# Turning the output and a token-major copy with VectorE's 32 x 32 transpose and 128-byte DMA pieces, instead of TensorE, in a fused attention and token/channel mixing kernel

## The chip, the cores and the metric

One Trainium2 chip, one core of it. The metric is the device time of one execution in microseconds (us); lower is better. The engines are written as in the profile: PE is TensorE, DVE is VectorE, ACT is ScalarE, POOL is GpSimd and SP is SyncE, which here issues nearly all DMAs.

## The reference

Two parts, one behind the other. Each of B = 8 batches has 8 heads, 1152 positions and head width 64. Queries are averaged in pairs, so there are 576 pooled queries per head.

```python
q_pool = q.reshape(B, H, S // 2, 2, D).mean(axis=3)
scores = matmul(q_pool, k^T) / sqrt(D)
attn = softmax(scores)                       # sum + 1e-9
x = (attn @ v) as [B, 576, H * D = 512]

theta = x @ w_theta                          # [576, 512] per batch
zr, zi = x * cos(theta), x * sin(theta)
y = w_tok_r @ zr + w_tok_i @ zi              # mixes the 576 tokens
u = x + y
out = u + max(u @ w_ch, 0)                   # mixes the 512 channels
```

Everything is float32. The kernel splits operands into a rounded high part and a rest (`hi` and `lo`, `xh` and `xl`, two `wth`, two `wtk`, two `wch`, two `us`) and multiplies three combinations, to keep float32 accuracy with a rounded format.

## The kernel before

**Phase 1** runs 32 pairs i = (batch b, head pair hp), two heads at a time, some 25 us each, to about 835 us. For pair i PE computes the score maxima (`pm`, L537; DVE reduces each with L544), the scores (`pe`, L622; ACT takes the exponential, L625), the sums of the exponentials (POOL adds them up, L636; PE collapses them in `pn`, L685) and the product with v (`pa`, L657; ACT copies it to `xu`, L669). `xu` is channel-major: 128 channels of two heads on the partitions, 576 tokens along the row. SP stores it to a DRAM tensor `xd[b]` (`norm_store`, L751). The copy of the row sums `sm` (L695, L697) goes to DRAM too (`norm_spread`, `sd<-sm`, L707), is inverted there in small tiles, and comes back as `rd`.

The schedule is written out by hand: `at(position, priority, function)` makes a list of steps, 18 units per pair, which is sorted, and each engine runs its instructions in the order of the list. A pair begins with a burst (`u = 0`): `prep_all` makes the operands of pair i + 2 (ACT `hi`, DVE `lo`, L524), then PE runs the products with v of the pair's first half. On DVE a weight-preparation step (`ws` L789, `wf` L791) stands behind `lo` in 18 of the pairs, and then come the pair's max reduces (`mx<-pm`).

PSUM in phase 1 is one pool of four two-bank tiles with tag `e`, so each new tile waits for the reader of the tile four allocations before it.

**Phase 2** handles the 8 batches in sequence with a period of some 57 us, again in an order written out by hand (`at2`, 56 units per batch). Per batch: `xT` (x by channel) is loaded from `xd`, scaled by the reciprocal sums (`xscale`, L240, with `dn` loaded from `rd`) and split into `xh` and `xl`. For each of up to five blocks j of 128 tokens `theta` (L297) runs 12 matmuls, and `xturn` (L285) turns the block of `xT` to token-major with four PE transposes into another PSUM bank; `chain` copies that to `xn` on ACT (L331), forms sine and cosine on DVE and ACT (`r`, `ab`), multiplies them with `xn` on DVE (L343), and rounds the products into `Z` (ACT L368, POOL L374). `token_mix` (L1055) multiplies the token weights with Z. `uadd` (L1071) adds x on DVE, giving `uT`, channel-major; `uhi` and `ulo` (L1077, L1081) split it into the tiles `us`; `channel` (L1096) multiplies with `wch`, and `relu` (L1108) adds the positive part into `uT`.

The output is wanted token-major. `oturn` (L1119) turns `uT` with 20 PE transposes per batch (five token blocks, four channel blocks) into PSUM, `ocopy` (L1137, ACT) copies it to SBUF, and `ostore` (L1143) writes whole rows to the output. For batches 0 to 6 these steps stand between the matmuls of the next batch.

Of the kernel before, what the change touches and what calls it, by code (L numbers as in the profile page):

```python
# [62 lines left out]
PAIRS = {"e": 4}  # L63
# [35 lines left out]
OT_AT = (58.2, 58.21, 58.22, 69.55, 69.56)  # L99
OT_AT6 = (58.2, 58.21, 58.22, 65.0, 65.01)  # L100
OT_LAG = (1.0, 1.0, 4.3, 1.0, 1.0)
OT_BANK = "rrtrr"
OT_LAST = "htmmr"
CH_LAST = ("mr", "mr", "mm", "mh")
CH_BANK = "mrmr"
TINY = 2.0**-15
# [9 lines left out]
def pooled_attention_moe_kernel(  # L116
# [50 lines left out]
    xd = [dram.tile([DM, SQ], F32, name=f"xd{b}") for b in range(B)]  # L167
    sd = [dram.tile([2 * H, HALF], F32, name=f"sd{b}") for b in range(B)]
# [5 lines left out]
    def bank2(kind, name):  # L174
        return ps.tile([P, 2, 512], F32, tag=kind, name=name, bufs=PAIRS[kind])

# [46 lines left out]
    def dload(b, c):  # L223
        if b == 1:
            if c == 0:
                shape = [P, H // 2, SQ]
                bst[b]["dns"] = pools["up"].tile(shape, F32R, tag="us0", name="dn1", bufs=1)
            dn = bst[b]["dns"][:, c].bitcast(F32)
        else:
            dn = dnp.tile([P, 5 * P], F32, tag="dn", name=f"dn{b}_{c}", bufs=2)  # L230
# [19 lines left out]

    chains = itertools.count()

    def turned(b, j):
        turn = bst[b].setdefault("turn", {})
        if j not in turn:
            if b == 0 and j < AHEAD:
                both = bank2("e", f"pq{j}")
                turn[j] = both[:, 0], both[:, 1]
            else:
                n = TURN0.index(j) - AHEAD  # L260
                th = bank("mhr"[n] if b == 0 else "h", f"pth{b}_{j}")
                turn[j] = th, bank("mtr"[n] if b == 0 else "t", f"pxn{b}_{j}")
# [39 lines left out]
    def chain(b, j):  # L302
# [27 lines left out]
        xn = tmp("xn")  # L330
        nc.scalar.copy(xn, st["xn", j])  # L331
# [52 lines left out]
    with ExitStack() as p1:  # L384
# [24 lines left out]
        if WARM:  # L409
            warm = bank2("e", "pwarm")  # L410
            for n in range(WARM):
                nc.tensor.matmul(warm[:, n % 2, 0:P], ident, ident, start=True, stop=True)

        state = {}

# [60 lines left out]
        def prep_t(i, g):  # L476
            st = state[i]
            kn = st["kn"]
            pt = st["pt", g] = bank2("e", f"pt{g}_{i}")
# [48 lines left out]
        def maxpass(i):  # L528
# [4 lines left out]
            for j in range(4):  # L533
                for g in range(3):
                    pm = bank2("e", f"pm{i}_{j}{g}")
# [10 lines left out]
                    )  # L546
                    yield

        def max_tail(i, pt):
            st = state[i]  # L550
            hi, tl, mx = st["hi"], st["tail"], st["mx"]
            pm = bank2("e", f"px{i}")
# [5 lines left out]
            if pt is None:  # L558
                pt = bank2("e", f"py{i}")
# [5 lines left out]
        def max_tail_red(i):  # L565
# [3 lines left out]
            nc.vector.tensor_reduce(mx[:, 8, 2:3], st["pt8"][:, 0, 3 * P :], AX.X, ALU.max)  # L569

# [19 lines left out]
        def first_row(i):  # L590
            px = bank2("e", f"pmt{i}")
            max_row(i, px)
            max_copy(i, px)

# [10 lines left out]
        def escore(i, u, kt):  # L605
# [4 lines left out]
            pe = bank2("e", f"pe{i}_{u}{kt}")  # L610
# [14 lines left out]
            nc.scalar.activation(pcs[u, kt], pe[:, :, 0:HALF], AF.Exp, scale=SC)  # L625

# [23 lines left out]
        def av(i, u):  # L650
# [3 lines left out]
            pa = bank2("e", f"pa{i}_{u}")  # L654
# [15 lines left out]
            if more:  # L670
                max_copy(i + 1, pa)

        def norm_sum(i, px):
# [22 lines left out]
            else:  # L696
                nc.scalar.activation(sm, px[:, 1, 0:HALF], AF.Identity, bias=eps)  # L697

# [26 lines left out]
        def prep_all(i, g):  # L725
# [5 lines left out]
            if g == 1:  # L731
                prep_tail(i)

        def tail_prep(i):
# [10 lines left out]
            if more:  # L745
                prep_lo(i + 3, 0)

# [7 lines left out]
        def weights():  # L755
# [79 lines left out]
            def finish_token(raw, kb, jt):  # L835
# [4 lines left out]
                pw2 = bank2("e", "pwt")  # L840
# [16 lines left out]
                for dst, src in (  # L857
# [6 lines left out]
                    split(dst[0], dst[1], src, nc.scalar, nc.vector)  # L864

# [62 lines left out]
        def plan(i):  # L928
# [42 lines left out]
            for n, fn in (  # L971
# [3 lines left out]
                at(base + pl[n], 9, fn, i)  # L975

        for i in range(NPAIR):
            plan(i)
        at(NU * NPAIR + 2, 9, lambda: norm_sum(NPAIR - 1, bank2("e", "pend")))
# [32 lines left out]
    with ExitStack() as p2:  # L1012
        for n, kinds in enumerate(BANKS2):
            both = bank2("e", f"pf{n}")
# [48 lines left out]
        def uadd(b, c):  # L1063
            st = bst[b]
            if c == 0:
                st["u"] = up.tile([P, ND, SQ], F32, tag="uT", name=f"uT{b}", bufs=1)
                for n in range(2):
                    st["us", n] = up.tile([P, ND, SQ], F32R, tag=f"us{n}", name=f"us{n}{b}", bufs=1)
# [6 lines left out]
        def uhi(b, c):  # L1075
            st = bst[b]
            nc.scalar.copy(st["us", 0][:, c], st["u"][:, c])  # L1077

        def ulo(b, c):
            st = bst[b]  # L1080
            engine("ulo", 1).tensor_tensor(  # L1081
                st["us", 1][:, c], st["u"][:, c], st["us", 0][:, c].bitcast(F32), ALU.subtract
# [168 lines left out]
```

## Time and profile before

| | |
|---|---|
| Median of 3 runs | 1301.83 us (1301.79 to 1302.61) |
| Span of the profiled execution | 1299.6 us |
| Clock of PE | 0.999 of full speed |
| Busy: PE, DVE, ACT, POOL | 1285.5, 854.9, 710.9, 902.8 us |
| DMA packets, of them under 512 B | 156774, 119878 |
| Share of the 16 DMA engines' time, main queue | 39.2% |

The span goes from the first to the last instruction of the profiled execution. The profiler gives no separate device time for that execution, so the median of the runs stands for it: it is 2.2 us above the span, which is the work around the first and the last instruction. The chain is followed back from the last instruction and names at each moment the engine and the line that the end waited for. The share of an engine's busy time says nothing by itself about a stage; phase 1 and phase 2 load POOL, DVE and ACT very differently.

### The profile page before, as it was taken

The page shows a single profiled execution, that of the slowest core. Times are in us where ns is not written, and L with a number is a line of the kernel's source. Part 1 is how long each engine was busy: PE and PEld are TensorE (multiplying, and loading weights), DVE is VectorE, ACT ScalarE, POOL GpSimd, SP SyncE. Part 2 cuts the span into 40 slices and gives each one's busy share as a digit, 9 for nine tenths or more (in the row PEclk, how much of TensorE's full clock was granted, in tenths as well). Part 3 has the DMA queues.
Part 4 walks back from the last instruction along what each step waited for, and adds up shares of the span by engine and source line. Part 5 has one row for each costly group of instructions (what it writes and reads, how often), then busy time and mean ns, then how long its engine had stood idle before and what let it go on. Part 6 is the DMA issues. An engine that isn't in the chain of part 4 may idle for free.

```text
span 1299.6 us, 30002 instructions
## 1 busy us (share of the span) xinstructions
PE 1285.5 (99%) x12165; PEld 1069.0 (82%) x12165; DVE 854.9 (66%) x1096; ACT 710.9 (55%) x1260; POOL 902.8 (69%) x669
## 2 busy tenths in 40 slices
PE   8999999999999999999999999999999999999998
PEld 6777777777777777777777777799999999999998
DVE  6677776867777786787778877676455454636432
ACT  4566666566566656656665665655345344435330
POOL 5899999999999999999999998424141324323220
PEclk9999999999999999999999999999999999999999
DMA  7446644644654563466448311223122221213011
GB/s 165 118 109 166 164 110 124 161 137 111 169 141 111 147 168 107 120 171 157 102 119 209 105 47 47 86 74 102 32 92 73 58 64 55 82 37 101 18 37 37
DMA packets 156774, 137.64 MB, mean 106 GB/s; under 512 B 119878, under 2 KB 120268, under 8 KB 156188
## 3 DMA queue, kind: packets, MB, share of 16 engines
q1 hardware_dynamic: 156144, 134.66, 39.2%
q8 instruction: 96, 1.57, 0.6%
q10 hardware_dynamic: 252, 0.60, 0.2%
q0 software_dynamic: 240, 0.46, 0.1%
q14 instruction: 42, 0.34, 0.1%
HBM read 104.96 MB, written 37.94 MB: 110 GB/s over the span
## 4 chain that ended last, share of the span: by engine, by line
PE 94%; DVE 3%; ACT 1%; DMA 1%; issue 0%; ACTq 0%; SPq 0%; POOL 0%; POOLq 0%; DVEq 0%
PE pe L622 25%; PE pa L657 22%; PE pf L1055 16%; PE pf L1096 8%; PE pf L297 7%; PE pm L537 5%; PE pt L492 4%; PE pn L685 2%; PE pf L1119 1%; PE px L554 1%; PE pf L285 1%; DVE mx L544 1%; DMA kn<-in_k_dram 1%; PE pq L297 0%; PE pwt L845 0%; PE pa L577 0%
## 5 line engine op out<-in xcount | busy, mean ns | idle before, releaser
L636 POOL TENSOR_TENSOR ss<-ss,pc 128x576 f32<-128x576 f32 x372 | 543.8, 1462 | 32.0 <-ACT pc L625 6.3
L544 DVE TENSOR_REDUCE mx<-pm 128x2 f32<-128x768 f32 x384 | 358.8, 956 | 167.6 <-PE pm L537 167.4
L625 ACT ACTIVATE pc<-pe 128x576 f32<-128x576 f32 x576 | 348.0, 651 | 52.2 <-PE pe L622 32.0
L657 PE MATMUL pa<-pc,vn 128*64 128x288 f32 x2304 | 294.4, 409 | 0.1
L657 PEld LDWEIGHTS pa<-pc,vn 128*64 128x64 f32 x2304 | 159.5, 137 | 107.0 <-issue 1.8
L374 POOL TENSOR_TENSOR Z<-ab,Z 128x512 fp32r<-128x512 f32 x35 | 46.9, 1341 | 281.2 <-ACT Z L368 237.8
L1055 PE MATMUL pf<-wtk,Z 128*128 128x288 f32 x1728 | 234.6, 295 | 0.8 <-ACT Z L368 0.8
L1055 PEld LDWEIGHTS pf<-wtk,Z 128*128 128x128 f32 x1728 | 230.9, 188 | 2.6 <-ACT Z L368 1.1
L622 PE MATMUL pe<-hi 64*128 64x288 f32 x1152 | 190.4, 327 | 0.9 <-DVE mx L544 0.8
L622 PE MATMUL pe<-nmr,oner 64*128 64x288 f32 x1152 | 170.4, 291 | 0.8 <-DMA nmr<-mT 0.7
L622 PE MATMUL pe<-hi,lo 64*128 64x288 f32 x1152 | 170.2, 291 | 0.0
L622 PE MATMUL pe<-lo,hi 64*128 64x288 f32 x1152 | 170.2, 292 | 0.0
L622 PEld LDWEIGHTS pe<-hi 64*128 64x128 f32 x1152 | 107.9, 184 | 45.3 <-issue 20.0
L537 PE MATMUL pm<-hi 64*128 64x384 f32 x826 | 127.3, 341 | 1.9 <-ACT hi L506 1.7
L669 ACT COPY xu<-pa 128x288 f32<-128x288 f32 x64 | 25.5, 399 | 156.7 <-PE pa L657 120.8
L622 PEld LDWEIGHTS pe<-nmr,oner 64*128 64x128 f32 x1152 | 108.6, 184 | 1.3 <-DMA nmr<-mT 1.3
L622 PEld LDWEIGHTS pe<-lo,hi 64*128 64x128 f32 x1152 | 108.9, 185 | 0.0
L622 PEld LDWEIGHTS pe<-hi,lo 64*128 64x128 f32 x1152 | 108.5, 185 | 0.0
L1096 PE MATMUL pf<-us,wch 128*128 128x288 f32 x768 | 105.4, 296 | 0.0
L1096 PEld LDWEIGHTS pf<-us,wch 128*128 128x128 f32 x768 | 104.0, 189 | 1.6
L636 POOL TENSOR_TENSOR ss<-pc,pc 128x576 f32<-128x576 f32 x62 | 90.9, 1466 | 0.7 <-ACT pc L625 0.7
L537 PEld LDWEIGHTS pm<-hi 64*128 64x128 f32 x826 | 76.5, 184 | 7.3 <-ACT hi L506 1.9
(161 smaller groups left out, 1633.8 us busy)
## 6 DMA issues: line engine op xcount, KB each, us to landing
vn<-in_v_dram SPq DMA_DIRECT2D x32, 576.0 KB
qn<-in_q_dram SPq DMA_DIRECT2D x31, 576.0 KB
kd<-in_k_dram SPq DMA_DIRECT2D x28, 576.0 KB
kn<-kd SPq DMA_DIRECT2D x56, 288.0 KB
xd<-xu SPq DMA_DIRECT2D x32, 288.0 KB
xT<-xd SPq DMA_DIRECT2D x8, 1152.0 KB
qp<-qn SPq DMA_DIRECT2D x56, 144.0 KB
dn<-rd SPq DMA_DIRECT2D x32, 160.0 KB
```

The source lines that it names most:

```text
L297: nc.tensor.matmul(th, xs[:, c, j * P : (j + 1) * P], ws[:, c], start=(n == 0), stop=(n == 11))
L374: eng.tensor_tensor(Z[1], t, Z[0].bitcast(F32), ALU.subtract)
L492: nc.tensor.transpose(out=dst, in_=src.rearrange("p h d -> p (h d)"), identity=unit)
L537: nc.tensor.matmul(pm[:, h, 0:W], hi[hs, Q0 + j * P : Q0 + (j + 1) * P], hi[hs, K0[3 * g] : K0[3 * g] + W], start=True, stop=True,)
L544: nc.vector.tensor_reduce(mx[:, j : j + 5 : 4, g : g + 1], pm[:, :, 0:W], AX.X, ALU.max)
L622: nc.tensor.matmul(pe[:, h, 0:HALF], w[hs], x[hs], start=(n == 0), stop=(n == 3))
L625: nc.scalar.activation(pcs[u, kt], pe[:, :, 0:HALF], AF.Exp, scale=SC)
L636: nc.gpsimd.tensor_tensor(st["ss", u], first, st["pc"][u, kt], ALU.add)
L657: nc.tensor.matmul(pa[hs, 0, 0:HALF], st["vn"][:, h, kt, :], st["pc"][u, kt][:, h, :], start=(kt == 0), stop=(kt == KT - 1),)
L685: nc.tensor.matmul(px[a : a + 32, 1, 0:HALF], ones, sets[u][n][:, h, :], start=(n == 0), stop=(n == len(sets[0]) - 1), tile_position=(0, a),)
L1055: nc.tensor.matmul(st["py", c, u][:, 0:HALF], Z[zi][:, c * P : (c + 1) * P], wtk[wi][:, kw, u * HALF : (u + 1) * HALF], start=(i == 0 and ...
L1096: nc.tensor.matmul(st["pr", e][u][:, 0:HALF], wch[wi][:, c, e * P : (e + 1) * P], st["us", ui][:, c, u * HALF : (u + 1) * HALF], start=(k ...
```

## The change

**Output.** For batches 0 to 6 `oturn`, `ocopy` and `ostore` are gone. `flip` runs four DVE transposes per batch, one for each channel block. The instruction turns square blocks of 32 x 32 within a [128 x 576] tile; so within 32 channels the tokens come to the partitions and the channels to the row, in runs of 32 elements. `fstore` then issues four DMAs for each of the four tiles, 576 pieces of 128 bytes each. Batch 7 stays as it was.

**Token-major copy.** For pairs 4 to 31 `xflip` turns `xu` in place on DVE, in the burst of the next pair, and `xstore` stores it to a new DRAM tensor `xs[b]` with four DMAs of 576 pieces of 128 bytes. In phase 2, for batches 1 to 7, `xnload` loads the blocks with rows of 2 KB, `rsload` loads the reciprocal sums token by token, 1024 elements of four bytes for each block, and `xnscale` multiplies the two on POOL. `xturn` and the ACT copy `xn` are left out for these batches, 31 blocks (b, j) in all. Batch 0 stays as it was.

**PSUM.** The four buffers become four tags of one buffer each, and the slot is chosen in the program: `bank2` takes the slot that was released first in program order, and `done` releases one. The tiles `pq0` and `pq1` of the last pair, which hold batch 0's first theta, are never released before phase 2. The tiles `us0` and `us1` are cut in halves.

```diff
-PAIRS = {"e": 4}
+RING = 4
-OT_AT = (58.2, 58.21, 58.22, 69.55, 69.56)
-OT_BANK = "rrtrr"
+FLIP_AT = (58.0, 59.0, 60.0, 61.0)
+STORE_LAG = 0.1
+XS_AT = 30.5
+XS_END = 2.5
+XN_LEAD = 9.0
+XN_LAG = 2.0
+RS_AT = -60.0
...
-    def bank2(kind, name):
-        return ps.tile([P, 2, 512], F32, tag=kind, name=name, bufs=PAIRS[kind])
+    slots = list(range(RING))
+    held = {}
+
+    def bank2(name):
+        n = slots.pop(0) if slots else held.pop(next(iter(held)))
+        held[name] = n
+        return ps.tile([P, 2, 512], F32, tag=f"e{n}", name=name, bufs=1)
+
+    def done(name):
+        slots.append(held.pop(name))
...
+    def rsload(b):
+        rs = bst[b]["rs"] = pools["up"].tile([P, 5, H], F32, tag="rs", name=f"rs{b}", bufs=2)
+        for j in range(5 if b % 2 == 0 else 4):
+            nc.sync.dma_start(
+                rs[:, j].rearrange("p (h o) -> p h o", o=1),
+                rd[b][:, j * P : (j + 1) * P].rearrange("h (p o) -> p h o", o=1),
+            )
...
+    def xnload(b, j):
...
+        if j < 4:
+            nc.sync.dma_start(xn, xs[b][j * P : (j + 1) * P])
...
+    def xnscale(b, j):
...
+        nc.gpsimd.tensor_tensor(xn, xn, rs.broadcast_to([P, H, D]), ALU.mult)
...
-        xn = tmp("xn")
-        nc.scalar.copy(xn, st["xn", j])
+        if b:
+            xn = st["xs", j]
+        else:
+            xn = tmp("xn")
+            nc.scalar.copy(xn, st["xn", j])
...
             if u == 0:
                 if 0 < i < NPAIR - 2:
                     prep_all(i + 2, 1)
+                if i > NP:
+                    xflip(i - 1)
                 whole_sum(i - 1, 1)
                 av(i, u)
                 if i > 0:
-                    norm_sum(i - 1, bank2("e", f"pn{i}"))
+                    norm_sum(i - 1, bank2(f"pn{i}"))
...
+        def xflip(i):
+            xu = state[i]["xu"].rearrange("p u c -> p (u c)")
+            nc.vector.transpose(out=xu, in_=xu)
+            xus[i] = xu
+
+        def xstore(i):
+            b, hp = divmod(i, NP)
+            src = xus.pop(i).rearrange("p (k f) -> p k f", f=32)
+            dst = xs[b].rearrange("(k r) e -> r k e", r=32)
+            for g in range(4):
+                c0 = hp * P + 32 * g
+                nc.sync.dma_start(dst[:, :, c0 : c0 + 32], src[32 * g : 32 * g + 32])
...
+        def flip(b, e):
+            st = bst[b]
+            if e % 2 == 0:
+                st["ots"] = up.tile([P, 2, SQ], F32, tag=f"us{e // 2}1", name=f"ot{b}_{e}", bufs=1)
+            ot = st["ot", e] = st["ots"][:, e % 2]
+            nc.vector.transpose(
+                out=ot.rearrange("p (n t f) -> p n t f", n=3, t=QT),
+                in_=st["u"][:, e].rearrange("p (t r n) -> p n t r", t=QT, n=3),
+            )
+
+        def fstore(b, e):
+            ot = bst[b]["ot", e].rearrange("p (m f) -> p m f", f=32)
+            ov = out[b].rearrange("(r m) e -> r m e", r=32)
+            for g in range(4):
+                c0 = e * P + 32 * g
+                nc.sync.dma_start(ov[:, :, c0 : c0 + 32], ot[32 * g : 32 * g + 32])
...
-            for j in range(0 if last else 5):
-                t = base + (OT_AT if b < B - 2 else OT_AT6)[j]
-                at2(t, oturn, b, j)
-                at2(t + OT_LAG[j], ocopy, b, j)
-                at2(t + OT_LAG[j] + 1, ostore, b, j)
+            for e in range(0 if last else ND):
+                at2(base + FLIP_AT[e], flip, b, e)
+                at2(base + FLIP_AT[e] + STORE_LAG, fstore, b, e)
```

PE, where the output of batch 0 ends and a theta of the next batches begins. `Z_8` is the last token block of a pair of batches, `uT` the output, `xT` the next x. Before:

```order
L1055 MATMUL pf_12649<-wtk_81,Z_8_13354 128x288 x2
L1055 MATMUL pf_12646<-wtk_81,Z_8_13353 128x288 x2
L1055 MATMUL pf_12646<-wtk_82,Z_8_13353 128x288 x2
L1055 MATMUL pf_12646<-wtk_81,Z_8_13354 128x288 x2
L1119 MATMUL pf_12648<-ident,uT_12964 128x128 x4
L1119 MATMUL pf_12648<-ident,uT_12964 64x128 x4
L285 MATMUL pf_12647<-ident,xT_10577 128x128 x4
L297 MATMUL pf_12647<-wth_79,xh_13443 128x512 x4
L297 MATMUL pf_12647<-wth_79,xl_13444 128x512 x4
L297 MATMUL pf_12647<-wth_80,xh_13443 128x512 x4
```

After the change (line 1126 is `token_mix`, line 334 `theta`):

```order
L1126 MATMUL pf_12797<-wtk_81,Z_8_13498 128x288 x2
L1126 MATMUL pf_12794<-wtk_81,Z_8_13497 128x288 x2
L1126 MATMUL pf_12794<-wtk_82,Z_8_13497 128x288 x2
L1126 MATMUL pf_12794<-wtk_81,Z_8_13498 128x288 x2
L334 MATMUL pf_12795<-wth_79,xh_13597 128x512 x4
L334 MATMUL pf_12795<-wth_79,xl_13598 128x512 x4
L334 MATMUL pf_12795<-wth_80,xh_13597 128x512 x4
```

The twelve transposes between `token_mix` and `theta` are gone and nothing has come in their place on PE.

DVE at the start of a pair in phase 1, where the pair has a weight-preparation step. `lo` belongs to the pair after next, `mx` to the next. Before:

```order
L574 TENSOR_REDUCE nm_6772<-mx_6470 128x9
L524 TENSOR_TENSOR lo_6601<-pt_18_6777,hi_6600 128x960
L789 TENSOR_SCALAR ws<-ws 128x576
L791 TENSOR_SCALAR wf<-ws 128x576
L544 TENSOR_REDUCE mx_6858<-pm_00_6859 128x2
```

After the change:

```order
L620 TENSOR_REDUCE nm_6835<-mx_6529 128x9
L566 TENSOR_TENSOR lo_6664<-pt_18_6840,hi_6663 128x960
L804 STREAM_TRANSPOSE xu_6475<-xu_6475 128x576
L856 TENSOR_SCALAR ws<-ws 128x576
L858 TENSOR_SCALAR wf<-ws 128x576
L586 TENSOR_REDUCE mx_6922<-pm_00_6923 128x2
```

The transpose stands ahead of the weight step and of the pair's first max reduce.

SP in one pair of phase 1 (`nmr` are the row maxima, `vn`, `qp` and `kn` the operands to come, `sd` the row sums). Before:

```order
L601 DMA nmr_170<-mT_6438 1x4x128 x2
L603 DMA nmr_170<-mT_6438 1x16x4 x2
L464 DMA vn_6466<-in_v_dram 128x2x576
L707 DMA sd_96<-sm_6449 4x288
L458 DMA qp_6907<-qn_6695 96x6x64 x2
```

After the change:

```order
L648 DMA nmr_179<-mT_6877 1x4x128 x2
L650 DMA nmr_179<-mT_6877 1x16x4 x2
L506 DMA vn_6907<-in_v_dram 128x2x576
L757 DMA sd_104<-sm_6888 4x288
L813 DMA xs_96<-xu_6475 32x18x32 x4
L836 DMA raw<-in_moe_w_tok_i_dram 32x1152
L836 DMA raw<-in_moe_w_tok_i_dram 96x1152
L500 DMA qp_6975<-qn_6758 96x6x64 x2
```

The four stores stand behind the row sums and ahead of the loads of the pairs to come.

## Rows read from the trace of the kernel before

**Rows 1.** The page: the span, busy time by engine.

```profile
span 1299.6 us, 30002 instructions
PE 1285.5 (99%) x12165; PEld 1069.0 (82%) x12165; DVE 854.9 (66%) x1096; ACT 710.9 (55%) x1260; POOL 902.8 (69%) x669
```

**Rows 2.** The chain, part of one batch of phase 2: start us, us, what.

```profile
902.93 1.31 PE pf L1119 x12
904.24 11.11 PE pf L1055 x84
915.36 0.87 PE pf L1119 x8
916.23 0.44 PE pf L285 x4
916.66 2.78 PE pf L297 x12
```

**Rows 3.** Groups by line: what | busy us, mean ns | idle before.

```profile
L1119 PE MATMUL pf<-ident,uT 128*128 128x128 f32 (+1 forms) x160 | 20.1, 273 | 0.0
L285 PE MATMUL pf<-ident,xT 128*128 128x128 f32 x136 | 20.7, 275 | 0.0
L331 ACT COPY xn<-pf 128x512 f32<-128x512 f32 x34 | 19.9, 586 | 35.1 <-DVE r L325 35.1
```

**Rows 4.** Stretches: from:to, length, busy us (instructions) by engine, clock, DMA share, GB/s.

```profile
306.00:308.00 2.00, 2.00 (x20) 1.17 (x18) 1.90 (x2) 0.35 (x1) 1.92 (x2) 1.00 1.02 197
300.00:400.00 100.00, 99.99 (x1106) 76.33 (x1104) 74.92 (x85) 62.62 (x115) 96.03 (x70) 1.00 0.54 135
1000.00:1050.00 50.00, 50.00 (x358) 48.40 (x358) 23.48 (x42) 20.78 (x36) 15.76 (x11) 1.00 0.27 77
```

**Rows 5.** DVE as a pair starts, twice: start us, us, what [idle before].

```profile
318.83 1.16 DVE L524 TENSOR_TENSOR lo<-pt,hi 128x960 fp32r<-128x960 f32 x1 [1.85 <-ACT hi L506]
...
322.63 0.96 DVE L544 TENSOR_REDUCE mx<-pm 128x2 f32<-128x768 f32 x1
...
397.48 0.96 DVE L544 TENSOR_REDUCE mx<-pm 128x2 f32<-128x768 f32 x1 [0.53 <-PE pm L537]
```

**Rows 6.** PE in the first of these two pairs.

```profile
323.66 0.38 PE L622 MATMUL pe<-hi 64*128 64x288 f32 x2
```

**Rows 7.** DVE groups by line that bear on the new operation.

```profile
L1081 DVE TENSOR_TENSOR us<-uT,us 128x576 fp32r<-128x576 f32 x32 | 28.0, 890 | 1.0 <-ACT us L1077 0.8
L789 DVE TENSOR_SCALAR ws<-ws 128x512 f32<-128x512 f32 (+2 forms) x18 | 18.2, 1009 | 0.0
L323 DVE TENSOR_SCALAR kk<-kk 128x512 f32<-128x512 f32 x36 | 16.4, 455 | 60.5 <-ACT kk L321 60.4
```

**Rows 8.** SP's issues within one pair of phase 1.

```profile
325.51 1.39 SPq L458 DMA_DIRECT2D qp<-qn  x2
327.00 3.50 SPq L433 DMA_DIRECT2D kn<-kd  x2
...
334.14 1.02 SPq L421 DMA_DIRECT2D qn<-in_q_dram  x1
346.26 1.39 SPq L601 DMA_DIRECT2D nmr<-mT  x2
```

**Rows 9.** DVE in phase 2, where one batch ends.

```profile
1032.37 1.55 DVE L1071 TENSOR_TENSOR uT<-xT,pf 128x288 f32<-128x288 f32 x4 [11.01 <-PE pf L1119]
1034.08 0.76 DVE L1081 TENSOR_TENSOR us<-uT,us 128x576 fp32r<-128x576 f32 x1 [0.16 <-ACT us L1077]
```

**Rows 10.** The chain at the last pair's end.

```profile
823.89 3.92 PE pe L622 x56
827.81 4.51 PE pa L657 x36
834.03 1.14 ACT Z L368 x2
```

**Rows 11.** ACT at the same place.

```profile
824.65 3.96 ACT L625 ACTIVATE pc<-pe 128x576 f32<-128x576 f32 x7 [0.20 <-PE pe L622]
```

More of the change, by code (lines that the diff above doesn't have):

```diff
@@ L167, in pooled_attention_moe_kernel @@
     xd = [dram.tile([DM, SQ], F32, name=f"xd{b}") for b in range(B)]
+    xs = [dram.tile([SQ, DM], F32, name=f"xs{b}") for b in range(B)]
     sd = [dram.tile([2 * H, HALF], F32, name=f"sd{b}") for b in range(B)]
@@ L224, in dload @@
         if b == 1:
[L225 to L228, printed above, removed]
+            if c % 2 == 0:
+                bst[b]["dns"] = pools["up"].tile(
+                    [P, 2, SQ], F32R, tag=f"us0{c // 2}", name=f"dn1_{c}", bufs=1
+                )
+            dn = bst[b]["dns"][:, c % 2].bitcast(F32)
         else:
@@ L249, in xload @@
             nc.sync.dma_start(xT[:, :, SQ : 5 * P], xv[:, :, 4 * P : SQ])
+    def rsload(b):
[5 more added lines that the diff above has]
+            )
+    loads = itertools.count()
+    def xnload(b, j):
+        side = ("xe", "ang")[next(loads) % 2]
+        xn = bst[b]["xs", j] = pools[side].tile([P, DM], F32, tag="xn", name="xn", bufs=1)
+        if j < 4:
+            nc.sync.dma_start(xn, xs[b][j * P : (j + 1) * P])
+        else:
+            for n in range(2):
+                nc.sync.dma_start(xn[n * HT : (n + 1) * HT], xs[b + n][j * P : j * P + HT])
+    def xnscale(b, j):
+        xn = bst[b]["xs", j].rearrange("p (h d) -> p h d", h=H)
+        rs = bst[b]["rs"][:, j].rearrange("p (h o) -> p h o", o=1)
+        nc.gpsimd.tensor_tensor(xn, xn, rs.broadcast_to([P, H, D]), ALU.mult)
     chains = itertools.count()
@@ L256, in turned @@
             if b == 0 and j < AHEAD:
-                both = bank2("e", f"pq{j}")
+                both = bank2(f"pq{j}")
                 turn[j] = both[:, 0], both[:, 1]
@@ L261, in turned @@
                 th = bank("mhr"[n] if b == 0 else "h", f"pth{b}_{j}")
-                turn[j] = th, bank("mtr"[n] if b == 0 else "t", f"pxn{b}_{j}")
+                turn[j] = th, bank("mtr"[n], f"pxn{b}_{j}") if b == 0 else None
         return turn[j]
@@ L329, in chain @@
         yield
-        xn = tmp("xn")
-        nc.scalar.copy(xn, st["xn", j])
+        if b:
+            xn = st["xs", j]
+        else:
+            xn = tmp("xn")
+            nc.scalar.copy(xn, st["xn", j])
         yield
@@ L569, in max_tail_red @@
             nc.vector.tensor_reduce(mx[:, 8, 2:3], st["pt8"][:, 0, 3 * P :], AX.X, ALU.max)
+            done(f"px{i}")
+            if f"py{i}" in held:
+                done(f"py{i}")
         def max_nm(i):
@@ L697, in norm_sum @@
                 nc.scalar.activation(sm, px[:, 1, 0:HALF], AF.Identity, bias=eps)
+            done("pend" if last else f"pn{i + 1}")
         def whole_sum(i, u):
@@ L975, in plan @@
                 at(base + pl[n], 9, fn, i)
+            if i >= NP:
+                at(base + (XS_AT if i < NPAIR - 1 else NU + XS_END + 0.01), 9, xstore, i)
         for i in range(NPAIR):
             plan(i)
-        at(NU * NPAIR + 2, 9, lambda: norm_sum(NPAIR - 1, bank2("e", "pend")))
+        at(NU * NPAIR + 2, 9, lambda: norm_sum(NPAIR - 1, bank2("pend")))
+        at(NU * NPAIR + XS_END, 9, xflip, NPAIR - 1)
         pw = ExitStack()
@@ L1013, in pooled_attention_moe_kernel @@
         for n, kinds in enumerate(BANKS2):
-            both = bank2("e", f"pf{n}")
+            both = bank2(f"pf{n}")
             for m, kind in enumerate(kinds):
@@ L1066, in uadd @@
                 st["u"] = up.tile([P, ND, SQ], F32, tag="uT", name=f"uT{b}", bufs=1)
-                for n in range(2):
-                    st["us", n] = up.tile([P, ND, SQ], F32R, tag=f"us{n}", name=f"us{n}{b}", bufs=1)
             for u in range(2):
@@ L1076, in uhi @@
             st = bst[b]
-            nc.scalar.copy(st["us", 0][:, c], st["u"][:, c])
+            if c % 2 == 0:
+                for n in range(2):
+                    st["us", n, c // 2] = up.tile(
+                        [P, 2, SQ], F32R, tag=f"us{n}{c // 2}", name=f"us{n}{b}_{c}", bufs=1
+                    )
+            nc.scalar.copy(st["us", 0, c // 2][:, c % 2], st["u"][:, c])
         def ulo(b, c):
@@ L1116, in oturn @@
             if 0 in es:
-                st["po", j] = bank((OT_LAST if b == B - 1 else OT_BANK)[j], f"po{b}_{j}")
+                st["po", j] = bank(OT_LAST[j], f"po{b}_{j}")
             for e in es:
@@ L1133, in ocopy @@
             st["on", j] = on
-            if b == B - 1 and j % 2:
+            if j % 2:
                 nc.vector.tensor_copy(on[0:R], st["po", j][0:R])
@@ L1165, in pooled_attention_moe_kernel @@
                 at2(PLAN2["wload"], wload)
+            else:
+                at2(max(base + RS_AT, 0.0), rsload, b)
             if b % 2:
```

47 lines of the change are left out of this document (31 added, 16 removed).

## The prediction

> **What bounds the kernel now.** I read the page first. PE is busy for 1285.5 of 1299.6 us [rows 1], so the question for every edit is whether PE does less, or is made to wait. I then read the chain of waits in phase 2, because a busy PE could still be one that others pace. In phase 2, behind its start, it is PE without a gap: each piece starts where the one before ended, and the turns that the change removes lie in it as pieces of their own [rows 2]. The reader is to see that 902.93 + 1.31 is 904.24, and so on down to the theta at 916.66. Third, the busy time in stretches. In phase 2 PE is busy for 50.00 of 50 us, and DVE, ACT and POOL for less than half. In phase 1 PE is as full (99.99 of 100), but POOL stands at 96 and DVE at 75, and the DMA engines at 0.54 [rows 4]. So work can be moved to DVE and DMA cheaply in phase 2; in phase 1 it depends on the place. Last I read DVE and SP row by row at the places where the order puts new instructions.
>
> **What is removed.** A batch's output turns stand in the chain as 1.31 us (12 matmuls) and 0.87 us (8), together 2.18 us [rows 2]. Seven batches give 15.3 us. A turn of one block of x stands there as 0.44 us for four matmuls [rows 2]; 31 blocks give 13.6 us. The groups by line count 160 and 136 such matmuls with a mean of 273 and 275 ns [rows 3]; these means overlap in the pipeline, so I don't multiply them: 0.44 / 4 = 0.11 us is what one costs the chain. Sum: 28.9 us off PE. ACT loses 31 + 35 copies of 586 ns [rows 3], which is off the path and counts as nothing; were it cover for something, it could only help.
>
> **What is added in phase 1: the transpose.** 28 times DVE turns a 128x576 tile in place, right behind `lo` and ahead of the weight step and of the next pair's first max reduce. That reduce frees the PSUM buffer that a `pe` four allocations later takes: the reduce of 322.63 ends at 323.59, and the `pe` starts at 323.66 [rows 5, 6]. So a delay of the reduce by more than 0.07 us arrives at PE. What absorbs it is DVE's idle time just before that reduce. I went through this place in all pairs. Most have 1.3 to 4.5 us of idle time there, three have about 1.0, and hide any price below. Seven have a weight step and little idle time: three have none, as at 322.63, one 0.29, three about 0.54, as at 397.48 [rows 5].
>
> The trace has no transpose on DVE. The nearest rows are these. One-input operations on 128x512 take 455 ns at L323, which scaled to 576 columns is 0.51 us. A subtraction of two 128x576 tiles that nothing disturbs takes 0.76 us [rows 9], and 890 ns in the mean of its line [rows 7]. The one-input operation of L789, which runs in phase 1 beside a POOL that is nearly always busy, takes 1009 ns in the mean [rows 7], 1.97 times the 0.51; the subtraction stretched alike would be 1.50 us. I take 0.76 us: one element per lane and step, as in the subtraction. Then three pairs lose 0.76 - 0.07 = 0.69 us each, one loses 0.40, three lose 0.15 each: 2.1 + 0.4 + 0.4 = 2.9 us. With 0.51 us it is three times 0.44 and once 0.15, 1.5 us. With 1.50 us it is three times 1.43, once 1.14, three times 0.89 and three times about 0.4: 9.3 us. These are the bounds, 1.5 and 9.3.
>
> The Trainium skill ("VectorE: DVE Perf Modes", section "The three transpose paths") gives 311 ns for a 128x128 bf16 transpose on VectorE. Four and a half of them would be 1.40 us, an estimate by that page, with which the sum below would come out about 5 us higher. No row here shows it.
>
> **What is added in phase 1: the stores.** Four DMAs per pair with 576 pieces each. SP takes 1.39 us to issue two DMAs of 576 pieces (`qp<-qn`), so four cost about 2.8 us. They stand behind `sd` and push `qp`, `kn`, `kd`, `xd` and `qn` of the pair back by that. SP then is idle from 335.16 to 346.26, when the next `nmr` comes [rows 8], so these 11 us absorb it before anything that PE waits for soon. PE turns `qp` and `kn` in later bursts. On the DMA engines the piece is the price. With only 256-byte pieces under way the engines were full at 197 GB/s [rows 4]: 16 x 256 / 197 = 21 ns per piece and engine. If a 128-byte piece costs between half of that (by bytes) and the same (by piece), 4 x 576 / 16 = 144 pieces per engine are 1.5 to 3.0 us in a pair of 25.1 us, at most 0.12 on a share of 0.54 [rows 4]. I count nothing.
>
> **What is added in phase 2.** Four transposes per batch on DVE, 4 x 0.76 = 3.0 us, stand where DVE was idle for 11.01 us, waiting for PE [rows 9]. The `uadd` behind them wants the next batch's token sums, later than that. POOL's scaling of 31 blocks falls into a POOL that is busy for 16 of 50 us. SP issues 16 output stores (16 x 0.70 = 11 us) and four or five `rs` loads (1024 pieces, by the `kn<-kd` row of two times 1152 pieces in 3.50 us [rows 8] some 1.55 us each, 7.8 us): 19 of about 53 us. DMA engines: 576 pieces per engine and batch for the output and up to 320 for `rs`, at 21 ns 18.8 us, beside 0.27 x 57 = 15 us now [rows 4]: 34 of 53 us. All of it fits; I count nothing. The cover is DVE's gap; if it were gone, the four transposes would cost up to 3 us in each of seven batches.
>
> **PSUM.** By the code nearly every allocation keeps its distance of four. It differs where `pq0` and `pq1` are held: in the last pair three slots are left, then two. There ACT's exponentials run at 3.96 us for seven [rows 11], 0.56 us each, next to PE's 56 matmuls in 3.92 us [rows 10]. With two slots a `pe` can only start when the exponential two before it has ended, so the pace goes from about 0.56 to about 0.7 us for the last seven tiles: 7 x 0.14 = 1.0 us. It reaches the ACT step that begins the way into phase 2 at 834.03 [rows 10]. Bounds 0 and 2. A few allocations at the very start change too, by some tenths in both directions; I count zero.
>
> **The sum.** 1299.6 - 15.3 - 13.6 + 2.9 + 1.0 = 1274.6 us of span. The profiled span lies 2.2 us below the median of the runs, 1301.83, so 1276.8 us, 1.9% less. Bounds of the forecast itself: with 1.5 and 0 us for the two losses 1274.4; with transposes of the 890 ns of L1081 (3.8 us) and 2 us in PSUM 1278.7.
>
> **Rivals.**
> *Transposes that POOL slows.* For: the same kind of instruction takes 1009 ns at L789 in phase 1 and 455 ns at L323 [rows 7], and POOL is 96% busy there [rows 4]. Against: the slow rows are of another operation, and the max reduces beside the same POOL take a steady 0.96 us [rows 5]. Price: 9.3 instead of 2.9 us, so 1283 us. The Trainium skill ("SBUF — State Buffer", section "SBUF: two separate sides") says that VectorE in a two-port mode, or with two SBUF inputs, and GpSimd lock each other out for whole instructions; it does not say which of these a transpose is.
>
> *Phase 2 gives part back.* The rows of xn stand in SP's queue among the output stores, and these wait for DVE's transposes at the end of the batch; so a product on DVE (L343) may wait for xn, then Z, then PE. It decides where xn lands later than the sine is ready; a delay of 1 us behind each of seven batches gives +7 us, so 1284 us. Against: xn is asked for 9 units ahead, and SP has half of each batch to spare.
>
> *The other side: the small pieces pace phase 2.* 15 us plus 896 pieces per engine have to fit into 53 us. They do up to 42 ns per piece, twice the 21 ns of the 256-byte pieces [rows 4]. At 46 ns the whole gain is eaten up (15 + 41 = 56 us per batch), at 50 ns a batch takes 60 us and the kernel 1276.8 + 7 x 7 = 1326 us. Against: reads of 256 bytes ran at 21 ns, and nothing in the trace shows a piece that costs more. The Trainium skill ("DMA: Bandwidth & Descriptors", section "Specifications") speaks against the change: below 512 bytes a transfer misses line rate, with a read-modify-write. The trace agrees in part, 197 GB/s with 256-byte pieces; no row shows what a write of 128 bytes costs.
>
> *The change doesn't do what it says:* the turns cost PE nothing, since something else would have held it there, 1302 us. The gapless chain [rows 2] speaks against it.
>
> **How the numbers follow.** Chances: the forecast 0.72, slowed transposes 0.12, phase 2 giving part back 0.08, small pieces 0.05, no effect 0.03. The predicted time is that of the forecast, 1276.8 us. The range goes from 1271 (bounds of the forecast less 3 us for waits at the old turns that I can't see) to 1287 (both losing rivals with some addition); it leaves out small pieces and no effect, and a tenth of the rest. About 0.2%, 2.6 us, is what a measurement of this kernel tells from no change. Faster by more: 0.72 + 0.12 + 0.08 = 0.92; within it 0.03; slower 0.05.
>
> **What the profile after will show.** No PE transposes of uT outside batch 7 and none of xT outside batch 0, with phase 2 about 29 us shorter and a period near 53 us. Transposes of 0.5 to 1.5 us on DVE; in phase 1 PE waits for a max reduce at some seven pairs, and phase 1 is about 3 us longer. In the last pair `pe` waits for ACT. Wrong would be: PE idle in phase 2 behind DVE, Z or SP; a DMA share near 1; or transposes above 1.5 us.

## The result and the profile after

The changed kernel takes 1278.35 us (median of 4 runs, 1277.28 to 1279.61) against 1301.81 us of the kernel before in the same runs. The ratio is 0.982, with a 95% interval of 0.9806 to 0.9834: 23.5 us less. 1276.8 us were forecast. The profiled execution has a span of 1276.0 us, 2.35 us under the median. Rows of the page:

```profile
PE 1259.6 (99%) x11901; PEld 1039.6 (81%) x11901; DVE 905.5 (71%) x1152; ACT 676.9 (53%) x1194; POOL 942.4 (74%) x700
...
DMA packets 321095, 154.15 MB, mean 121 GB/s; under 512 B 284262, under 2 KB 284652, under 8 KB 320508
...
q1 hardware_dynamic: 320464, 151.19, 49.8%
```

PE has 25.9 us less to do than in [rows 1], and its share is the same: it still sets the time. There are 164384 packets under 512 bytes more, and the queue's share is 49.8% instead of 39.2%.

The stages show where the time went. The marks are the starts of certain matmuls of PE in the two traces, in us: the first collapse of a pair's sums (`pn`), the last one (`pn` of pair 31 and `pend`), and the first channel matmul of batch 7.

| Up to | Before | After | Added in the stage | Forecast |
|---|---|---|---|---|
| first `pn` (start) | 68.82 | 69.74 | +0.92 | 0 |
| last `pn` (transposes, stores) | 823.19 | 824.74 | +0.63 | +2.9 |
| `pend` (last pair) | 832.26 | 835.48 | +1.67 | +1.0 |
| `channel` of batch 7 | 1278.80 | 1255.46 | -26.56 | -28.9 |
| the end | 1299.61 | 1275.99 | -0.28 | 0 |

These are two traces, and a stage is not the same in every execution. From the first to the last `pn` the changed kernel took 755.00 us here; in the eight traces e5 to e12 below, whose phase 1 has the same steps, it took 755.61 to 755.81 us. By those the transposes and stores add 1.2 to 1.4 us and not 0.63. The stage from `pend` to batch 7 is steadier: 419.98 us here, 419.49 to 420.23 us in e2, e3, e5 and e12, which leave phase 2 alone or almost so.

The chain of waits in the stretch that [rows 2] showed (line 1126 is `token_mix`, 334 `theta`, 1173 `channel`):

```profile
902.62 14.28 PE pf L1126 x108
916.89 2.79 PE pf L334 x12
919.69 7.93 PE pf L1126 x60
927.61 2.81 PE pf L334 x12
...
930.44 0.70 ACT kk L358
...
931.17 0.96 DVE kk L360
...
938.74 0.83 DVE uT L1140 x2
...
939.70 3.39 PE pf L1173 x24
```

The turns are gone: token mixing runs for 14.28 us in one piece, with theta right behind it. But a new part has come. At 930.4 the chain leaves PE for ACT and DVE and comes back at 939.70, where `channel` starts late. PE works on beside that part; it stands idle only for the last 0.16 us of it. The new groups by line, and three groups that changed beside them (line 856 is the `ws` of L789, 1155 the `us` of L1081, 360 the `kk` of L323, [rows 7]):

```profile
L1227 DVE STREAM_TRANSPOSE ot<-uT 128x576 f32<-128x576 f32 x28 | 24.7, 941 | 0.0
L804 DVE STREAM_TRANSPOSE xu<-xu 128x576 f32<-128x576 f32 x28 | 21.6, 770 | 1.7 <-DMA xd<-xu 1.6
L856 DVE TENSOR_SCALAR ws<-ws 128x512 f32<-128x512 f32 (+2 forms) x18 | 13.4, 743 | 0.0
L1155 DVE TENSOR_TENSOR us<-uT,us 128x576 fp32r<-128x576 f32 x32 | 31.4, 996 | 0.1
L360 DVE TENSOR_SCALAR kk<-kk 128x512 f32<-128x512 f32 x36 | 18.9, 524 | 53.7 <-ACT kk L358 53.6
```

A transpose takes 770 ns in phase 1 and 941 ns in phase 2, where its input is read with a stride and it writes to another tile; no run tells the two apart. `ws` went from 1009 to 743 ns, `kk` from 455 to 524, and `us` from 890 to 996. None of these three was changed.

### The profile page after: what moved, and what is told of

Same layout as the page of the kernel before. It is cut to its first block, busy times and chain, and to the rows that moved or that the text cites. A ratio compares the mean times of both kernels' runs of the same rounds, so it can differ in the third digit from the quotient of the medians.

```text
span 1276.0 us, 29808 instructions
## 1 busy us (share of the span) xinstructions
PE 1259.6 (99%) x11901; PEld 1039.6 (81%) x11901; DVE 905.5 (71%) x1152; ACT 676.9 (53%) x1194; POOL 942.4 (74%) x700
## 3 DMA queue, kind: packets, MB, share of 16 engines
q1 hardware_dynamic: 320464, 151.19, 49.8%
## 4 chain that ended last, share of the span: by engine, by line
PE 90%; DVE 4%; ACT 2%; POOL 1%; DMA 1%; issue 1%; ACTq 0%; SPq 0%; POOLq 0%; DVEq 0%
PE pe L669 24%; PE pa L705 21%; PE pf L1126 16%; PE pf L1173 8%; PE pf L334 6%; PE pm L579 5%; PE pt L534 3%; PE pn L734 2%; PE px L597 1%; DVE mx L586 1%; POOL ss L684 1%; DMA kn<-in_k_dram 1%; ACT pc L672 0%; PE pq L334 0%; ACT hi L548 0%
## 5 line engine op out<-in xcount | busy, mean ns | idle before, releaser
L566 DVE TENSOR_TENSOR lo<-pt,hi 128x768 fp32r<-128x768 f32 (+1 forms) x60 | 63.2, 1053 | 27.1 <-ACT hi L548 26.8
```

The lines of the kernel that those rows point to most:

```text
L566: nc.vector.tensor_tensor(lo, src, hi.bitcast(F32), ALU.subtract)
```

## The experiments

The times are medians. Each kernel was run beside the kernel before, whose medians lie from 1301.58 to 1301.89 us. The interval of a ratio reaches some 0.0014 to each side, 1.8 us; where two versions of the changed kernel differ by less or little more, the medians alone don't tell them apart, and the marks in the traces have to.

**e1_ring: the PSUM part undone.**

```diff
-        n = slots.pop(0) if slots else held.pop(next(iter(held)))
-        held[name] = n
-        return ps.tile([P, 2, 512], F32, tag=f"e{n}", name=name, bufs=1)
+        held[name] = 0
+        return ps.tile([P, 2, 512], F32, tag="e", name=name, bufs=RING)
```

> The changed kernel with PSUM as before (one tag with four buffers), all else as changed. Theory: the changed kernel loses 1.7 us in the last pair, where two slots are left, and about 0.6 us at the start, both by the fixed order of PSUM buffers. So 2.3 us less than the changed kernel's 1278.35 us: 1276.0 us, with seven exponentials of the last pair at 3.96 us again and the last pair's sums some 2.3 us earlier. Rival: both losses come from the added transfers and transposes; then the time stays at 1278 us and the last pair's exponentials stay at 0.8 us each.

Measured: 1348.2 us, ratio 1.0361 (1.0346 to 1.0375). Both theories fell. The start (68.89 us) and the last pair (9.16 us from `pn` to `pend`, before 9.07) were indeed as before, but between the sums `pn5` and `pn23` it lost 72 us. The table of waits, and the chain in one of these pairs (line 668 is `pe`, 671 the exponential):

```profile
PEld pe L668 <- ACT pc L671: 37.3, 58, 1.3
PEld pm L578 <- ACT pc L671: 24.8, 30, 1.1
```

```profile
173.14 0.82 PE pe L668 x8
...
174.04 0.66 ACT pc L671
...
174.75 0.82 PE pe L668 x8
...
175.65 0.66 ACT pc L671
```

PE and ACT take turns: a `pe` can't start before an exponential has ended. In the changed kernel the first of these waits is 3.2 us in 11 waits. In the program as built, the buffers of the pool with one tag are reused like this, from pair 5 on, where the first `xflip` stands (tile, tile before it in the same buffer, distance):

```
pe5_16  after pe5_14  3
pm7_02  after pe5_15  3
pe5_17  after pe5_16  2
pe5_18  after pe5_17  1
pm7_10  after pe5_18  1
```

So the fixed order is no loss with a small side effect, as I had it: without it the new steps of phase 1 cost 72 us. Not all of that is waiting. The granted clock between 170 and 700 us was 0.97 in the mean, where the changed kernel has 1.00; 3% of these 530 us are 16 us, so up to that much, an estimate, is slower matmuls. Without the transposes and the stores of phase 1 the pool's order is harmless: e4_output_only has it, leaves out both, and loses nothing in phase 1. The runs don't tell which of the two it takes, nor why the pool then chooses so.

**e2_no_xflip and e3_xflip_behind_w: what the transposes of phase 1 cost.** The first leaves out the line below; the second moves the call behind the weight step.

```diff
-            nc.vector.transpose(out=xu, in_=xu)
```

```diff
-                if i > NP:
-                    xflip(i - 1)
...
+            if i > NP:
+                at(base + 10.38, 4, xflip, i - 1)
```

> The changed kernel without the 28 transposes of xu in phase 1; xu is stored as it is, so the token-major copy holds other values. Theory: in front of ws the transpose fills time in which ws waited for POOL anyway, so phase 1 becomes shorter by about 0.6 us only (1277.7 us), and the mean of ws goes back from 743 to about 1009 ns. Rival, the sum of the prediction: 2.9 us less, 1275.5 us.

> The changed kernel with the transpose of xu behind the weight step (ws, wf) instead of ahead of it. Theory: ws waits for POOL again (mean near 1.0 us instead of 0.74) and the 0.77 us of the transpose come on top at the pairs without idle time, three times 0.7 and four times 0.1 to 0.4 us: about 2 us more than the changed kernel, 1280.4 us. Rival: DVE's idle time hides the transpose wherever it stands, 1278.4 us.

Measured: 1278.22 us without the transposes (0.9817, 0.9803 to 0.983) and 1279.34 us with them behind the weight step (0.9826, 0.9812 to 0.9839). By the medians, leaving them out gives 0.1 us and moving them costs 1.0 us; both lie within the intervals. From the first to the last `pn`, e2 took 754.15 us and e3 755.98 us. Beside the changed kernel's 755.00 us that makes the transposes worth 0.85 us and the move 1.0 us. Beside the 755.61 to 755.81 us of the eight later traces the transposes are worth 1.5 to 1.7 us and the move only 0.2 to 0.4 us. None of these reaches the 2.9 us of the prediction, nor the 2 us that I expected of e3. The mean of `ws` is 997 ns without the transposes and 981 ns with the transposes behind it, as against 743 ns behind a transpose (825 to 850 ns in the eight later traces). DVE at the place of [rows 5], in the changed kernel:

```profile
320.83 0.77 DVE L804 STREAM_TRANSPOSE xu<-xu 128x576 f32<-128x576 f32 x1
321.52 0.49 DVE L856 TENSOR_SCALAR ws<-ws 128x576 f32<-128x576 f32 x1
...
323.58 0.96 DVE L586 TENSOR_REDUCE mx<-pm 128x2 f32<-128x768 f32 x1
```

and in e3_xflip_behind_w:

```profile
320.89 1.10 DVE L854 TENSOR_SCALAR ws<-ws 128x576 f32<-128x576 f32 x1
...
323.50 0.77 DVE L802 STREAM_TRANSPOSE xu<-xu 128x576 f32<-128x576 f32 x1
324.19 1.78 DVE L586 TENSOR_REDUCE mx<-pm 128x2 f32<-128x768 f32 x2
```

In the one, transpose and `ws` take 0.77 + 0.49 us where before `ws` alone took 1.10 us: most of the transpose lies in time that `ws` had spent waiting. In the other `ws` takes its 1.10 us again, the transpose comes on top, and the max reduce starts at 324.19 instead of 323.58. What `ws` waits for is POOL: in the kernel before, 17 of the 18 `ws` end 0.28 to 0.32 us behind the end of the POOL instruction that was running when they began.

So what a transpose costs hangs on where POOL happens to stand when the `ws` behind it begins. At the first transpose, in pair 5, the changed kernel and e6_no_scale have the same steps in the same order. First the changed kernel, then e6:

```profile
170.65 0.42 DVE L856 TENSOR_SCALAR ws<-ws 128x576 f32<-128x576 f32 x1
```

```profile
170.41 1.62 DVE L856 TENSOR_SCALAR ws<-ws 128x576 f32<-128x576 f32 x1
```

In the first, `ws` began 0.03 us behind a POOL instruction and did not wait for it; in the second 0.12 us behind one, and waited it out. All eight later traces show the second (1.60 to 1.66 us), and there PE reaches the next pair's `pn` 1.0 us later. The profile of the changed kernel caught the cheap case.

**e4_output_only: the output part alone.** The kernel before with `flip` and `fstore`, nothing else; in terms of the changed kernel:

```diff
-                if b:
-                    at2(t - XN_LEAD, xnload, b, j)
-                    at2(t + XN_LAG, xnscale, b, j)
...
-                    if b == 0:
-                        at2(t, xturn, b, j)
+                    at2(t, xturn, b, j)
```

> The kernel before with the output part of the change alone (DVE transposes of uT and 128-byte stores); x is turned by PE and PSUM is as before. Theory: without POOL's scaling of xn nothing stretches DVE's work in phase 2, so the whole 15.3 us arrive: 1286.5 us, and no wait of PE above 0.1 us in phase 2. Rival: the transposes and stores at the end of each batch give part back themselves, 1288 us or more, with waits of channel or theta in phase 2.

Measured: 1286.09 us, ratio 0.9881 (0.9867 to 0.9894): 15.6 us less than before, where 15.3 were worked out. From the transposes and stores of the output nothing is given back.

**e5_release: the last pair.**

```diff
+            at(t + 0.0001, 3, done, f"pq{j}")
```

> The changed kernel with pq0 and pq1 released behind the copy that reads them last, so that the last pair has four slots again. Theory: the sums of the last pair start 9.1 instead of 10.7 us after those of the pair before, and the time falls by 1.7 us to 1276.7 us, since the way into phase 2 begins there. Rival: the start of phase 2 is set by loads or DVE; then the gain is lost behind it and the time stays at 1278.3 us.

Measured: 1276.91 us (0.9806, 0.9793 to 0.9819), 1.4 us less than the changed kernel. From `pn` to `pend` it is 9.15 us, as before, instead of 10.74. In the changed kernel the chain reads there (line 669 is `pe`, 672 the exponential, 705 `pa`):

```profile
827.00 0.82 PE pe L669 x8
...
827.91 0.66 ACT pc L672
...
828.61 0.82 PE pe L669 x8
```

and ACT beside it has two exponentials in a row, then a wait:

```profile
827.91 1.39 ACT L672 ACTIVATE pc<-pe 128x576 f32<-128x576 f32 x2 [0.21 <-PE pe L669]
```

From 827.00 to 828.61 are 1.61 us for two tiles, 0.80 each. That is the two slots: in e5 PE runs the 56 matmuls of the seven tiles in one piece of 3.92 us again, as in [rows 10].

**e6_no_scale and e7_dve_scale: what phase 2 gave back.** The first leaves out the call of `xnscale`; the second puts it on DVE, and later:

```diff
-XN_LAG = 2.0
+XN_LAG = 4.6
...
-        nc.gpsimd.tensor_tensor(xn, xn, rs.broadcast_to([P, H, D]), ALU.mult)
+        nc.vector.tensor_tensor(xn, xn, rs.broadcast_to([P, H, D]), ALU.mult)
```

> The changed kernel without the scaling of xn on POOL; xn is used as loaded, so the values differ. Theory: POOL's scaling stretches the DVE steps beside it (kk from 0.43 to 0.95 us, the two rests of us from 2.51 to 3.35 us), and these six places cost PE 2.2 us in phase 2; without it 1276.1 us and no wait of PE above 0.1 us between theta, token mixing and channel mixing. Rival: xn or the stores come late by themselves; then the waits of 0.2 to 0.5 us stay and so does the time, 1278.3 us.

> The changed kernel with the scaling of xn on DVE, between r and the products, where DVE is idle for 1.95 us waiting for ACT. Theory: a product of 128x512 takes 0.69 us there and is hidden, POOL stretches nothing, so about 1276.3 us. Rival: DVE gets late with the 21 us more and channel or theta wait longer: 1279 us or more.

Measured: 1275.74 us (0.9797, 0.9784 to 0.9811) and 1276.1 us (0.9802, 0.9789 to 0.9816). From `pend` to the channel matmuls of batch 7 both take 417.3 us, the changed kernel 419.98 and the kernel before 446.54. So 2.7 us were given back, and without POOL's scaling they are all there. The later place in e7 is not the reason, since e6 has the loads where they were and shows the same. Here is what POOL does while DVE's `kk` at 931.17 (chain above) takes 0.96 us:

```profile
930.79 2.23 POOL L286 TENSOR_TENSOR xn<-xn,rs 128x512 f32<-128x512 f32 x2
```

DVE at the same place in e7_dve_scale, and three of its groups by line:

```profile
930.48 0.43 DVE L360 TENSOR_SCALAR kk<-kk 128x512 f32<-128x512 f32 x1 [3.93 <-ACT kk L358]
...
932.73 0.68 DVE L286 TENSOR_TENSOR xn<-xn,rs 128x512 f32<-128x512 f32 x1
934.70 0.69 DVE L391 TENSOR_TENSOR kk<-xn,ab 64x512 f32<-64x512 f32 x1 [1.29 <-ACT ab L378]
```

```profile
L286 DVE TENSOR_TENSOR xn<-xn,rs 128x512 f32<-128x512 f32 x31 | 21.2, 684 | 0.0
L1155 DVE TENSOR_TENSOR us<-uT,us 128x576 fp32r<-128x576 f32 x32 | 28.0, 890 | 0.1
L360 DVE TENSOR_SCALAR kk<-kk 128x512 f32<-128x512 f32 x36 | 16.4, 456 | 57.5 <-ACT kk L358 57.1
```

`kk` and `us` have their old 456 and 890 ns. The scaling takes 684 ns in the time in which DVE waits for ACT anyway.

**e8_double_store, e9_scratch_store and e12_scratch_later: how near the small pieces are to pacing phase 2.** e8 issues each store twice. e9 sends the second one to a DRAM tensor that nobody reads, e12 does that 11 to 14 units later.

```diff
                 nc.sync.dma_start(ov[:, :, c0 : c0 + 32], ot[32 * g : 32 * g + 32])
+                nc.sync.dma_start(od[b].rearrange("(r m) e -> r m e", r=32)[:, :, c0 : c0 + 32], ot[32 * g : 32 * g + 32])
```

```diff
+                at2(base + 72.0 + 0.1 * e, sstore, b, e)
```

> The changed kernel with each of the 112 output stores issued twice (same data to the same place). The queue's share rose from 39.2% of 1299.6 us to 49.8% of 1276.0 us with 164384 more packets under 512 bytes, some 12 ns per piece and engine. Theory: 7 us more DMA time and 11 us more SP time per batch of 54 us are still hidden: within 1 us of 1278.3 us. Rival, that the stores are near to pacing phase 2 already (the prediction's other side): 2 us or more per batch, 1292 us or more.

> The changed kernel with a second store of each output tile to a DRAM tensor that nobody reads, so that the second store does not wait for the first one; again twice the pieces. What slowed the kernel with the doubled store by 206 us: by the waits (SP 188.9 us on out_dram in 112 waits), it was SP standing at each second store until the first had landed, with the loads of xn queued behind it. Theory: without these waits the doubled pieces are nearly hidden, within 3 us of the changed kernel (1278 to 1281 us). Rival: 128-byte pieces pace phase 2 by themselves; then 1300 us or more, with a DMA share near 1 in the stretches of the stores.

> The second stores to the unused DRAM tensor again, but 14 units later, so that they stand in SP's queue behind the row sums and the first xn loads of the batch and not between them and the output stores. The doubled pieces stay. In the run before, SP issued each store in 0.67 us while the DMA engines stood at 0.6, and the load of the row sums (rc) waited behind 16 stores more. Theory: SP's order and not the pieces cost the 27 us; so most of it goes, 1278 to 1284 us. Rival: the pieces themselves: 1300 us or more as before.

Measured: e8 1484.53 us (1.1402, 1.1386 to 1.1418), e9 1305.3 us (1.003, 1.0019 to 1.0042), e12 1279.63 us (0.9835, 0.9821 to 0.9849). In e8 SP waits for the landing of the first store before each second one:

```profile
SPq L1238 <- DMA out_dram<-ot: 188.9, 112, 3.2
```

That experiment measured the landing, not the pieces; it missed its question. e9 has no such wait, and my expectation of 1278 to 1281 us was still wrong. Its chain at the end of a batch (1238 and 1239 are the two stores, the middle of the sixteen left out; `rc` the row sums of the next batches, `uT` the next `uadd`):

```profile
909.71 0.69 SPq L1238
...
920.44 0.63 SPq L1239
921.12 2.01 DMA rc<-sd
...
923.45 0.76 DVE uT L1141 x2
924.26 0.85 PE pf L1127 x2
```

The load of `rc` stands in SP's queue behind 16 of the stores and is issued 11.4 us after the first of them; in the changed kernel it is 6.7 us. DVE waits for it with the reciprocal, and the `uadd` stands behind that on DVE. The DMA engines are not full meanwhile. PE is busy up to 920 and then stands idle for 4 of the next 5 us, and its granted clock falls to 0.74 in the mean of that stretch, which lengthens the loss (the columns are those of [rows 4]):

```profile
915.00:920.00 5.00, 5.00 (x31) 4.41 (x30) 0.00 (x0) 0.00 (x0) 0.00 (x0) 1.00 0.61 97
920.00:925.00 5.00, 1.03 (x5) 0.52 (x3) 1.78 (x5) 0.71 (x2) 0.00 (x0) 0.74 0.65 100
```

In e12 the same number of pieces is moved, but the second stores stand behind `rc` (which is the DMA at 915.98):

```profile
909.58 6.35 SPq L1238 DMA_DIRECT2D out_dram<-ot  x8
915.98 0.62 SPq L223 DMA_DIRECT2D rc<-sd  x1
...
927.18 11.74 SPq L1245 DMA_DIRECT2D od<-ot  x16
```

1.3 us more than the changed kernel for twice the output pieces, which is within the intervals; from `pend` to batch 7 it is 420.23 us, as in the changed kernel. Not the pieces, but what queues behind their issues on SP, is the cost.

**e10_both and e11_both_start: the improvements together.** e10 is e5 and e7. e11 also gives the first 110 PSUM tiles the slots that they had in the kernel before:

```diff
-        n = slots.pop(0) if slots else held.pop(next(iter(held)))
+        n = first.pop(0) if first else slots[0] if slots else None
+        n = slots.pop(slots.index(n) if n in slots else 0) if slots else held.pop(next(iter(held)))
```

> The changed kernel with pq0 and pq1 released and the scaling of xn on DVE. Theory: the two losses lie behind one another on PE's path, so the gains of 1.4 and 2.2 us add: 1274.7 us. Rival: phase 2 takes up the earlier end of phase 1 in another wait: 1276 us.

> As the one before, with the slots of the first 110 PSUM tiles in the order that the kernel before has. Theory: the wait of pe for an exponential at 48.79 us goes, and 0.5 to 0.9 us with it: 1274.0 us, with the first sums at 68.9 us instead of 69.4 to 69.7. Rival: the later start comes from the loads at the very beginning and stays: 1274.7 us.

Measured: 1274.28 us (0.9792, 0.9779 to 0.9805) and 1273.42 us (0.9786, 0.9773 to 0.9799). The gains add. In the changed kernel `pe` waits at the start for an exponential:

```profile
47.45 0.40 PE L669 MATMUL pe<-hi 64*128 64x288 f32 x2 [0.17 <-DVE mx L586]
...
48.79 0.40 PE L669 MATMUL pe<-hi 64*128 64x288 f32 x2 [0.54 <-ACT pc L672]
```

In e11 this wait is gone and the first `pn` stands at 68.90 us; with the slots of the changed kernel it stands at 69.27 to 69.74 us in nine traces and at 70.60 us in e10, whose profiled execution was its slowest. e1 and e4, which have the old slots, start at 68.89 and 69.02 us. e11 is the fastest version, 4.9 us below the changed kernel. Its gain on e10 is 0.9 us, within the overlap of the two intervals; the first `pn` is what shows it.

## Why the prediction was right, step by step

- **What bounds the kernel:** right. PE is busy for 99% before and after, and the turns that lay in the chain came off it.
- **The 28.9 us of turns:** right in size. The output part gave 15.6 us for 15.3 (e4_output_only). Without the scaling on POOL phase 2 is 29.2 us shorter (e7_dve_scale, 446.54 to 417.31 us).
- **"I count nothing" for phase 2:** wrong by 2.7 us. The step that failed is "POOL's scaling of 31 blocks falls into a POOL that is busy for 16 of 50 us". I asked whether POOL had time, and not what DVE does beside it. The rival that part is given back in phase 2 was right that something comes back and wrong on how: the late thing was not xn (in e6 its loads stay, and nothing is lost; in the changed kernel one product, at 1089.71, waits 2.31 us for xn, with no wait of PE behind it), but `kk`, `us` and the four `xl` at the start of phase 2 (3.33 us, in e7 2.48) were stretched. The Trainium skill ("SBUF — State Buffer", section "SBUF: two separate sides") has this rule, a lock between GpSimd and VectorE instructions with two SBUF inputs or in a two-port mode; the trace agrees, with `kk` at 0.96 us beside POOL and 0.43 us without.
- **The transposes, 2.9 us:** the duration was right (0.77 us for 0.76), the term was too large. It is 0.1 us by the medians, 0.85 us by the changed kernel's trace and 1.5 to 1.7 us by the eight later ones (e2). I took DVE's row of instructions as a sum of fixed durations. But `ws` behind the transpose had been waiting for POOL, and mostly became shorter when it came later: 743 ns in the mean, in the later traces 825 to 850, instead of 1009. The pairs that I charged were the wrong ones, too: the place at 322.63 cost next to nothing, and where the term came due it was pair 5, charged with 0.40 us, that cost 1.0.
- **Transposes that POOL slows** (rival): excluded. 28 transposes took 767 to 780 ns, with POOL at 96.03 of 100 us between 300 and 400 us, as in [rows 4]. Of the estimate by the Trainium skill ("VectorE: DVE Perf Modes", section "The three transpose paths"), 1.40 us, little more than half was measured.
- **PSUM, +1.0 us in the last pair:** right in place, too small: 1.67 us. I took 0.7 us for the pace with two slots; it was 0.80, as a `pe` and an exponential alternate with hand-overs between them. The start, counted as zero, cost 0.4 to 0.8 us through the slots (e11).
- **The stores of phase 1:** hidden, as said. The DMA share between 300 and 400 us went from 0.54 to 0.62.
- **The piece:** 10 to 21 ns were the bounds. By the queue's shares it is (0.498 x 1276.0 - 0.392 x 1299.6) x 16 / 164384 = 12 ns, a mean that holds the four-byte pieces of `rs` as well; the 129024 packets of 128 bytes in the trace take 13.1 ns each, and those of 256 bytes 22.0. So it is nearer to the bytes than to the piece. SP's part was overpriced: five `rs` loads, put at 7.8 us, took 3.60 us to issue (from 903.49 on). The other side, small pieces that pace phase 2, was argued with the wrong resource: at 128 bytes SP's 0.67 us per store comes first, and e9 shows that 16 stores more at the wrong place in SP's queue do eat up the whole gain. The Trainium skill's floor of 512 bytes for line rate ("DMA: Bandwidth & Descriptors", "Specifications") did not show as a cost of the kernel: in e12 twice the output pieces left phase 2 as long as it was.

The errors partly cancel. By the two traces they are 2.3 us too much for the transposes, against 2.7 us of POOL's scaling, 0.7 us in the last pair and 0.9 us at the start. That the total came within 1.5 us, nearer than its terms, is luck in part.

## What to carry to other kernels

When TensorE is the bound without a gap, its transposes can go to VectorE and to small DMA pieces at their full value; ask then of each new instruction not only whether its engine has time, but which instructions of VectorE and GpSimd it meets, and what queues behind it on the DMA issuer. Before a stall in a row of instructions is added up, look whether the next one's duration already holds a wait. What is read from one trace can be one case of several: look at the same stage in every trace that shares its steps. When a buffer pool chooses slots itself, look again after every change of order: the same work took 72 us longer in phase 1 by slots alone.

## What the runs showed of the hardware that I had not expected

The 32 x 32 transpose of VectorE keeps its time beside a busy GpSimd (767 to 780 ns), while a one-input float32 operation of the same shape, `ws`, varies from 421 to 1299 ns in the same trace. With a strided input, in phase 2, the transpose took 910 to 982 ns.

When PE stood idle in e8_double_store, its granted clock fell (from:to, length, busy PE, PEld, DVE, ACT, POOL, clock, DMA share, GB/s):

```profile
960.00:970.00 10.00, 0.00 (x0) 0.00 (x0) 1.84 (x2) 0.00 (x0) 2.04 (x2) 0.59 0.24 64
970.00:980.00 10.00, 7.33 (x30) 7.13 (x31) 8.44 (x16) 4.21 (x7) 1.28 (x1) 0.56 0.78 225
980.00:990.00 10.00, 10.00 (x66) 9.29 (x65) 6.71 (x12) 3.68 (x6) 4.73 (x4) 1.00 0.11 34
```

It was idle for the whole first stretch; the clock of that and the next one is 0.59 and 0.56 of full speed in the mean, near the lower of its two levels (1.2 GHz, where full speed is 2.4 GHz), and full again in the last. The first work behind the wait:

```profile
972.67 6.10 PE L1173 MATMUL pf<-us,wch 128*128 128x288 f32 x24 [12.95 <-DVE uT L1140]
```

In the changed kernel 24 such matmuls take 3.39 us (the chain above, at 939.70). A wait of PE of this length costs more than the wait itself.
